# Feature attention and a maxout network on one core: unit 0's k and q set up apart, maxima of q as a row from unit 2 on, and a new order table

## The chip, the cores and the metric

One core of one Trainium2 chip runs the whole kernel. Its engines are TensorE (PE in the profile, with PEld for its weight loads), VectorE (DVE), ScalarE (ACT), GpSimd (POOL) and SyncE (SP, which issues transfers). The metric is the device time of one execution in microseconds; of several runs the median is taken. The profiled execution has a time of its own, and its span, from the first to the last instruction, is a little shorter.

## What is computed

```python
def phi(x):                                   # x: 8 batches, 8 heads, 576 tokens, 64 channels
    proj = einsum('bhsd,df->bhsf', x, w_phi)  # 128 features
    proj = proj - max(abs(proj), axis=-1)
    return concatenate([exp(proj), exp(-proj)], axis=-1)
q_p, k_p = phi(q), phi(k)
kv = einsum('bhsf,bhsd->bhfd', k_p, v);  z = sum(k_p, axis=2)
num = einsum('bhsf,bhfd->bhsd', q_p, kv)
den = einsum('bhsf,bhf->bhs', q_p, z) + 1e-6
x = num / den                                 # heads side by side: 4608 tokens of 512
h = maximum(maximum(x @ w1, x @ w2), x @ w3)  # 512 to 768
out = h @ w_out                               # 768 to 512
```

Each token of q and of k is thus projected to 128 features, and the largest absolute projection of that token is taken off ahead of both exponentials. Matrix products are in bf16 with fp32 sums.

## The kernel before

**Units.** Four heads of one batch are a unit; there are 16 units, two to a batch. A unit holds 18 tiles of 128 tokens, worked in groups of four tiles and one group of two (GROUPS). attention(u) makes the steps of a unit, each with a kind that the code names:

- L: loads. Units 0 to 3 have q and k loaded by GpSimd's queue as bf16 (line 460), and later units in fp32 by SP's. Unit 0's k comes in two halves in fp32 by SP (449), and VectorE copies it to bf16 (453, kind C). v comes in fp32 by SP (471). For units 1 to 3 a gate stands ahead of v: a one-element copy on VectorE (469), without which SP's queue does not go on.
- T and Tc: tokens and channels are exchanged. In units 0 to 3 TensorE does this (491), for q and k of a tile in one step, into a PSUM bank, and a copy brings them to qkT (494): q's channels in partitions 0 to 63, k's in 64 to 127. Later units use a transposing DMA (506).
- G: the projections with w_phi, into one bank for q (psq) and one for k (psk) (533), q and k alternating; the last two tiles share one bank (528). w_phi itself is loaded twice by SP, once for each half of the partitions (407, 408), and VectorE copies it to bf16 (403, 404).
- ek and r: ScalarE takes the two exponentials of k's projections (546); VectorE takes the maxima of the absolute values (552) of k (mk) and of q (mqp).
- E, va, vd: ScalarE makes exp(-max) of k from mk (584); GpSimd scales v by it (588) to vab, one copy for each of the two exponentials, and a small copy adds the factor itself (598).
- M and eq: q's projections once more, now with features in partitions and the maximum already subtracted (bank psm), and their exponentials on ScalarE (626). The maximum is subtracted in one of two ways. By products: a first product (615), and one small product for each tile (618), whose weights are a column of maxima spread wide and whose other operand is minus the identity. By a row: TensorE turns the maxima (560, kind R), a copy (564) and a DMA (568, kind V) put them as one more row, number 64, into qkT, and one product of 65 rows with w_phi and a row of -1 does all (613). SUBT tells from which unit on the row is used. The DMA is issued by ScalarE's queue for units below V_ACT, and by SP's for the others.
- K, N, x, X: kv sums (642), their copies kv_sb (647), numerators and denominators (660), the division on VectorE (666, 667), and the turn to xT (680, 683).

The network works in chunks of 512 tokens: chunk() makes ups (713), the maximum in hT (719, 721, 723), and the output (741, 746, 754). Its weights come by GpSimd's queue (421) and are prepared in steps of their own: differences of weights (788), turned weights (800, 803), and the product of w1 and w_out (814, 818).

**What sets the order.** Every step is a Node with costs for each engine that may do it. The order is a table written out (PLAN): each word has the number of a node, a letter for the engine (T TensorE, D VectorE, A ScalarE, G GpSimd, S SyncE), the buffers that it takes, and a due time. plan() reads it and issues the nodes in the table's order, so each engine runs its steps strictly in that order; the due times do nothing on the chip, and the engines wait for each other by semaphores. fill() adds unread products: where the table leaves TensorE without a step for more than a given gap, it puts matmuls of a constant tile (idler, made at 846) into a free bank. They have no reader. WARM and SLOW tell fill() until when the smaller gap counts, and until when such products are spaced for 0.43 us each.

Of the kernel before, what the change touches and what calls it, by code (L numbers as in the profile page):

```python
# [42 lines left out]
SUBT = 4  # L43
HALVES = 1
WARM = 28.0
SLOW = 4.6
JOIN = 2
MOVE = 5
# [49 lines left out]
2D0@0.5 8S0@0.7 10S@1.3 4S@1.9 0G@0.5 6G0@1.1 7G@1.9 12S0@3.1 3D@0.8 9D@4.5 5D@5.5 11D@6.2 1G@2.8 1051G@3.2 13T1@5.9  # L98
14D0@6.7 82G1@4.0 83G@4.9 17T2@7.5 15T3@7.6 24T004500@8.0 19T67@8.4 18D@7.8 16D@8.3 22D@8.9 27D@9.5 29T12@9.1 39T3@9.3
34T64@10.3 32D@10.1 42D@10.7 37D@11.1 26A@8.6 25A@9.3 31A@9.7 21A@10.2 36A@10.9 35A@11.5 20A@12.0 33D@11.7 38D@12.3  # L100
43D@12.9 28D@13.2 23D@13.8 64T10@11.8 58T6@12.2 65A@12.5 66A@13.0 156G2@5.7 155G@6.6 1061T4@13.0 61T1@13.6 1065T0@14.1
55T5@14.7 52T7@15.2 41A@13.4 60A@13.7 48A0@14.2 62A@14.4 44A@14.9 59A@15.2 40A@15.7 53A@16.0 30A@16.5 57A@17.0
47A0@17.5 63A@17.6 56A@18.1 54A@18.6 49G@14.6 45G@15.7 1054G@16.8 1062D0@14.4 46G@17.6 51G@18.7 50G@19.0 1052G@20.1
84D1@15.6 1066D@15.7 86T4@16.4 90T6@16.9 88T3@17.1 87D1@17.2 89D@17.8 91D@18.4 92T110211@18.0 102T41@18.6 97T35@18.8
112T6@19.1 95D@18.6 96D@19.3 107T70@19.4 103A@19.1 113A@19.6 93A@20.0 108A@20.5 109A@21.1 85S@15.8 105D@19.9 110D@20.5
67T047@21.2 115D@21.1 100D@21.4 106D@22.0 94A@21.6 98A@22.1 104A@22.8 68A@23.3 128T31@22.3 1063T2@22.8 222G0@20.9
159T1@23.4 131T4@24.0 129A@23.7 116D@22.6 69D@23.0 111D@23.3 121A1@24.2 114A@24.4 123G1@24.6 124G@25.7 101D@24.0
137T7@24.6 130A@24.7 139A@25.2 117A@25.6 99A@25.8 138A@26.3 118G@26.0 119G@27.1 122G@28.2 125T0@24.8 132A@26.6
133A@27.3 120A@27.8 134T6@25.3 136A@27.9 135A@28.6 126A@29.0 127A@29.7 223G@29.3 76T30@25.8 1053G@30.2 1057G@31.0
1055G@33.1 1064D@24.6 160D2@25.7 74T2@26.1 70T5@26.5 77D0@26.3 71D1@27.0 75D0@27.6 1071T1@26.8 157D2@28.3 1072D@28.4  # L110
# [157 lines left out]
def fill(order, spare, make, ready):  # L268
# [8 lines left out]
    for n in order:  # L277
# [3 lines left out]
        while gap > (0.35 if t < WARM else 0.5) and t < n.start - 0.2:  # L281
            for i in range(len(pool.last)):
                if all(x[0] != i or x[2] < t - 0.1 or x[1] > t + 0.6 for x in spans.values()):
                    todo.append((t, make(i)))
                    spans[t] = [i, t, t + 0.5]
                    break
# [591 lines left out]
```

## Time and profile before

| | us |
|---|---|
| median of three runs | 293.51 |
| the three runs | 292.33, 293.51, 296.66 |
| profiled execution, its own time | 292.35 |
| its span | 290.6 |
| PE busy (unread products included) | 279.4 |
| ACT busy | 189.9 |
| DVE busy | 215.9 |
| POOL busy | 117.4 |

The span is the profile's zero point to its last instruction, and times of instructions are given from its start. Busy times are sums over the span. TensorE's instructions overlap, so that the time one of them takes is longer than the distance to the next; distances between starts tell what a matmul costs in a row of them. A line of the timeline has the start, the time, engine, source line, operation, what is written and read, the number of instructions merged, and in brackets the idle time ahead of it with what ended it. The profiled execution holds 23 unread products.

### The profile page before, as it was taken

The numbers are of one execution on the slowest core, as the hardware profiler recorded it, in microseconds if no ns is written. First come the engines' busy times: TensorE is split into PE (matmuls) and PEld (weight loads), VectorE is DVE, ScalarE is ACT, GpSimd is POOL, SyncE is SP. The second block draws the span as 40 slices with busy tenths as digits, with TensorE's granted clock in tenths as the row PEclk, the third lists the DMA queues.
The fourth block names the chain that finished last, engine by engine and source line by source line (L and its number), as shares of the span: only waits on it lengthen the run. The fifth ranks groups of instructions, "written<-read, shape, count | busy, mean of one in ns | idle before, by whom it ended". The sixth has DMA issues, their size and how long they took to land.

```text
span 290.6 us, 8659 instructions
## 1 busy us (share of the span) xinstructions
PE 279.4 (96%) x3602; PEld 158.7 (55%) x3641; DVE 215.9 (74%) x457; ACT 189.9 (65%) x438; POOL 117.4 (40%) x101
## 2 busy tenths in 40 slices
PE   8878999999999999999999999999999999999993
PEld 3556685646645585564466556545555564444442
DVE  2987999998876899768989959898796583242360
ACT  1599798977988899799669797566858631120101
POOL 8086886276093751552780519107064300000000
PEclk9999999999999999999999999999999999999999
DMA  7999988997967799796995779658534523500605
GB/s 191 208 201 181 218 249 271 230 335 178 356 132 258 221 189 279 165 287 130 298 182 106 173 235 206 138 126 174 102 107 95 112 21 72 126 18 2 144 18 128
DMA packets 63051, 49.87 MB, mean 172 GB/s; under 512 B 43556, under 2 KB 48036, under 8 KB 63012
## 3 DMA queue, kind: packets, MB, share of 16 engines
q1 hardware_dynamic: 58644, 44.04, 61.2%
q0 software_dynamic: 4288, 5.21, 11.0%
q8 instruction: 28, 0.46, 0.6%
q14 instruction: 11, 0.09, 0.1%
q10 hardware_dynamic: 80, 0.07, 0.1%
HBM read 34.67 MB, written 9.44 MB: 152 GB/s over the span
## 4 chain that ended last, share of the span: by engine, by line
PE 86%; DVE 6%; ACT 4%; DMA 2%; issue 1%; SPq 0%; ACTq 0%
PE ups L713 30%; PE ops L746 16%; PE ops L741 11%; PE kvps L642 7%; PE psn L660 6%; PE psq L533 5%; PE psm L613 4%; DVE mqp L552 2%; DMA wphi_f<-in_w_phi_dram 2%; DVE mk L552 2%; ACT Ek L546 2%; PE tps L491 1%; PE pxT L680 1%; PE psm L618 1%; PE psq L528 1%
## 5 line engine op out<-in xcount | busy, mean ns | idle before, releaser
L588 POOL TENSOR_TENSOR vab<-v_raw,em 128x1152 bf16<-128x1152 f32 (+1 forms) x36 | 68.2, 1907 | 88.7 <-ACT em L584 67.7
L713 PE MATMUL ups<-xT,w_bf 128*128 128x512 bf16 x411 | 100.7, 379 | 1.1
L546 ACT ACTIVATE Ek<-psk 128x512 bf16<-128x512 f32 x128 | 70.5, 607 | 23.7 <-PE psk L533 17.0
L626 ACT ACTIVATE Eq<-psm 128x512 bf16<-128x512 f32 (+1 forms) x160 | 79.2, 586 | 7.9 <-PE psm L613 6.2
L713 PEld LDWEIGHTS <-w_bf 128*128 128x128 bf16 x432 | 40.3, 98 | 44.1 <-DVE x_sb L667 0.2
L746 PE MATMUL ops<-wout_bf,hT 128*128 128x512 bf16 (+1 forms) x219 | 50.7, 373 | 0.3
L552 DVE TENSOR_REDUCE mqp<-psq 128x4 bf16<-128x512 f32 (+1 forms) x80 | 47.7, 631 | 2.0 <-PE psk L533 1.0
L719 DVE TENSOR_TENSOR hT<-hT,ups 128x512 bf16<-128x512 bf16 x54 | 35.9, 683 | 14.2 <-ACT hT L721 6.8
L552 DVE TENSOR_REDUCE mk<-psk 128x4 f32<-128x512 f32 x64 | 42.5, 681 | 1.7 <-ACT Ek L546 1.2
L746 PEld LDWEIGHTS <-hT 128*128 128x128 bf16 x222 | 21.3, 98 | 22.8 <-DVE hT L719 0.2
L721 ACT ACTIVATE hT<-ups 128x512 bf16<-128x512 f32 x28 | 16.4, 613 | 26.2 <-PE ups L713 26.1
L667 DVE TENSOR_TENSOR x_sb<-psn,rden 128x320 bf16<-128x320 f32 x64 | 31.5, 492 | 2.2
L660 PEld LDWEIGHTS <-Eq 128*128 128x128 bf16 x640 | 24.5, 97 | 6.5 <-issue 0.3
L754 DVE COPY osb<-ops 128x512 f32<-128x512 f32 (+1 forms) x19 | 12.6, 674 | 18.9 <-PE ops L746 18.9
L660 PE MATMUL psn<-kv_sb,Eq 128*128 128x65 bf16 x640 | 26.3, 193 | 0.1
L723 DVE TENSOR_SCALAR hT<-ups 128x512 bf16<-128x512 f32 x26 | 17.5, 686 | 11.4 <-PE ups L713 11.1
L754 ACT COPY osb<-ops 128x512 f32<-128x512 f32 (+1 forms) x18 | 10.3, 575 | 23.7 <-DMA out_dram<-osb 9.6
L741 PE MATMUL ops<-xT 128*128 128x512 bf16 x86 | 24.1, 380 | 0.5
L642 PEld LDWEIGHTS <-Ek 64*128 64x128 bf16 x1152 | 18.4, 94 | 5.7 <-issue 2.8
L642 PE MATMUL kvps<-vab,Ek 64*128 64x65 bf16 x1152 | 20.5, 190 | 0.9 <-POOL vab L588 0.5
L533 PE MATMUL psq<-w,qkT 64*128 64x128 bf16 x256 | 20.4, 217 | 0.4 <-DVE qkT L494 0.4
L533 PEld LDWEIGHTS <-qkT 64*128 64x128 bf16 x512 | 14.5, 94 | 10.7 <-issue 7.7
(72 smaller groups left out, 277.8 us busy)
## 6 DMA issues: line engine op xcount, KB each, us to landing
v_raw<-in_v_dram SPq DMA_DIRECT2D x16, 576.0 KB, 4.6
out_dram<-osb SPq DMA_DIRECT2D x70, 128.0 KB, 2.4
k_raw<-in_k_dram SPq DMA_DIRECT2D x12, 576.0 KB, 4.9
q_raw<-in_q_dram SPq DMA_DIRECT2D x12, 576.0 KB, 6.1
w_bf<-in_moe_w_dram POOLq DMA_DIRECT2D x3, 768.0 KB, 10.0
qk_bf<-in_q_dram POOLq DMA_DIRECT2D x3, 288.0 KB, 10.6
qk_bf<-in_k_dram POOLq DMA_DIRECT2D x3, 288.0 KB, 11.1
wout_bf<-in_moe_w_out_dram POOLq DMA_DIRECT2D x1, 768.0 KB, 9.5
```

Source lines behind the costliest of these rows:

```text
L533: nc.tensor.matmul(ps()[:, i, :], lhsT=cols[r, :], rhs=w2[r, c, :], start=True, stop=True)
L546: nc.scalar.activation(Ek[s]()[:, tiles_of(t0, n), :], of(1), EXP, scale=1.0 - 2.0 * s)
L552: nc.vector.tensor_reduce((mq, mk)[c]()[:, tiles_of(t0, n)], of(c), AXX, ALU.max, apply_absolute_value=True)
L588: (nc.vector if n_.eng == "DVE" else nc.gpsimd).tensor_tensor(vab()[:, g, t0:t1, 0:D], vb()[:, t0:t1, :], em()[:, g, t0:t1].unsqueeze(2).t ...
L626: nc.scalar.activation(Eqb()[s][:, cols], psm()[:, 0:w], EXP, scale=1.0 - 2.0 * s)
L642: nc.tensor.matmul(kvps[ab]()[:, t // NT, g, :], lhsT=Ek[g]()[r, t, :], rhs=vab()[r, g, t, :], start=(t + g == 0), stop=(t == UT - 1 and g ...
L660: nc.tensor.matmul(psn()[:, c, :], lhsT=Eqb()[g][:, t0:t0 + P], rhs=kv()[:, pr, ab, g, :], start=(g == 0), stop=(g == 1))
L667: nc.vector.tensor_tensor(x_sb()[:, pr, :, ab, :], psn()[:, :, 0:D], rden().to_broadcast([P, 5, D]), ALU.mult)
L713: nc.tensor.matmul(ups(), lhsT=w_bf[i + 1][:, ct, j * P:(j + 1) * P], rhs=tokens_of(ct), start=(ct == 0), stop=(ct == CT - 1))
L719: nc.vector.tensor_tensor(hT()[:, j, :], hT()[:, j, :], ups(), ALU.max)
L741: nc.tensor.matmul(ops_()[:, 0:width], lhsT=tile_of(ct, tt), rhs=line_w[c_i > MOVE][:, ct, cols], start=(ct == 0), stop=False)
L746: nc.tensor.matmul(ops_()[:, 0:width], lhsT=hT()[:, j, tt * P:(tt + 1) * P], rhs=wout_bf[:, j, cols], start=False, stop=(j == JT - 1))
```

## The change

- In unit 0, k's turn (T), its copy (Tc) and its projections (G) are steps of their own, apart from q's, in banks of their own; the copies may go to ScalarE, and the table has k's three copies there and q's three on VectorE. One of the two copies of k to bf16 goes to ScalarE as well. The last two tiles of q and k still share one projection step (G). Units 1 to 15 keep q and k together.
- w_phi is loaded by ScalarE's queue, the half that k's partitions use first, behind the load of the activation table. In VectorE's order its copies to bf16 come ahead of the cast of k's second half; before they came between the two casts.
- SUBT is 2 and not 4: units 2 and 3 subtract q's maxima by the row, with the DMA on ScalarE's queue.
- fill() counts smaller gaps (0.25 and not 0.35, until 34.0 and not 28.0), spaces its products by 0.22 and not 0.26 after SLOW, puts up to two more close ahead of a step that ends a gap of over 0.6, and lets one bank serve more of them. There are 38 unread products in the program and not 23; 16 stand ahead of the first transposes and not 13.
- The table is new throughout. In its first part, SP's queue has, after the two halves of unit 0's k, unit 1's v with its gate and then unit 0's v; before, unit 0's v came right behind w_phi. GpSimd's queue has q and k of unit 1 ahead of the first network weight (before, the weight was first), and q and k of unit 2 behind GpSimd's small copy of unit 0's first factors (before, ahead of it). ScalarE's first kv copies go to VectorE.

Of the diff, the table is cut to its first lines on both sides; the changed functions are whole.

```diff
--- before.py
+++ after.py
@@ -40,11 +40,12 @@
 XW = SM + P
 BY_PE = 4
 X_PE = 6
-SUBT = 4
+SUBT=2
 HALVES = 1
-WARM = 28.0
+WARM = 34.0
 SLOW = 4.6
 JOIN = 2
+TWO_BANKS = 99
 MOVE = 5
 VA_DVE = 1
 QK = 3
@@ -95,152 +96,153 @@
 PLAN = """
-2D0@0.5 8S0@0.7 10S@1.3 4S@1.9 0G@0.5 6G0@1.1 7G@1.9 12S0@3.1 3D@0.8 9D@4.5 5D@5.5 11D@6.2 1G@2.8 1051G@3.2 13T1@5.9
-14D0@6.7 82G1@4.0 83G@4.9 17T2@7.5 15T3@7.6 24T004500@8.0 19T67@8.4 18D@7.8 16D@8.3 22D@8.9 27D@9.5 29T12@9.1 39T3@9.3
...
+8S0@0.7 10S@1.3 2D0@0.5 4A@0.7 3D@0.8 0G@0.5 6G0@1.1 7G@1.9 92G1@2.8 5D@4.6 11D@6.1 1G@3.6 9A@4.5 19T1@5.9 13T2@6.2
+17T3@6.7 21T4@6.8 15T5@7.0 23T6@7.3 14A0@6.7 20D@6.5 16A@7.6 18A@8.6 22D@7.3 24D@7.9 32T07@7.3 31T0100@7.8 26T2@8.0
+38T4@8.2 44T6@8.4 36D@8.2 35D@8.8 41D@9.5 47D@10.1 43T5@8.7 37T3@9.1 49T7@9.6 25T4@10.2 46A@9.2 33A@9.7 51A@10.2
...
@@ -278,13 +280,16 @@
         if n.eng != "PE":
             continue
         gap, t = n.start - free, max(free + 0.1, ready)
-        while gap > (0.35 if t < WARM else 0.5) and t < n.start - 0.2:
+
+        late = 2 if gap > 0.6 and t < WARM else 0
+        while gap > (0.25 if t < WARM else 0.5) and (t < n.start - 0.1 or late):
+            if t >= n.start - 0.1:
+                t, late = n.start - 0.02 * late, late - 1
             for i in range(len(pool.last)):
-                if all(x[0] != i or x[2] < t - 0.1 or x[1] > t + 0.6 for x in spans.values()):
+                if all(x[0] != i or x[2] < t - 0.1 or x[1] >= n.start for x in spans.values()):
                     todo.append((t, make(i)))
-                    spans[t] = [i, t, t + 0.5]
                     break
-            t += 0.26 if t > SLOW else 0.43
+            t += 0.22 if t > SLOW else 0.43
         free = n.start + n.costs["PE"]
     return [fn for _, fn in sorted(todo, key=lambda x: x[0])]
 
@@ -404,8 +409,8 @@
         nc.vector.tensor_copy(wphi_m[0:D, :], wphi_f[0:D, :])
 
     def phi_load():
-        nc.sync.dma_start(wphi_f[0:D, :], w_phi)
-        nc.sync.dma_start(wphi_f[D:2 * D, :], w_phi)
+        nc.scalar.dma_start(wphi_f[D:2 * D, :], w_phi)
+        nc.scalar.dma_start(wphi_f[0:D, :], w_phi)
 
     n_ident = node("const", 0, {"POOL": 0.55}, lambda: make_identity(nc, ident), [], [])
     n_minus = node("const", 0, {"POOL": 0.5}, lambda: nc.gpsimd.tensor_scalar_mul(minus, ident, -1.0), [n_ident], [])
@@ -413,8 +418,9 @@
     spare = bank("spare", [P, SM])
     n_idle = node("const", 0, {"DVE": 0.2}, lambda: nc.vector.memset(idle, 1.0), [], [spare])
     n_const = node("const", 0, {"DVE": 2.2}, zeros, [n_idle], [])
-    n_phi = node("phi", 0, {"SP": 1.2}, phi_load, [], [], pipe=0.05, lat=2.0, dmas=2)
+    n_phi = node("phi", 0, {"ACT": 1.2}, phi_load, [], [])
     n_phi = node("phi", 0, {"DVE": 0.7}, phi_weights, [n_phi, n_const], [])
+    n_phi.after = 4.6
 
     def w_load(i):
         dst = (w_bf + [wout_bf])[i]
@@ -477,27 +483,37 @@
             cast[c, 0] = nd("C", {"POOL": 0.13 + 0.055 * UT}, lambda c=c: nc.gpsimd.tensor_copy(
                 qk()[:, :, c * D:(c + 1) * D], raw_bufs(u)[c]()), [mains[c]], [(qb, kb)[c], qk])
 
-        tr = {}
+        tr, tr_of = {}, {}
 
         def tiled(t):
             return t.rearrange("p (t c) -> p t c", c=P)
         if by_pe:
-            for i, (t0, nb) in enumerate(BATCHES):
-                tps = bank("tps", [P, 8, P], BF16)
-
-                def tp(t0=t0, nb=nb, tps=tps):
-                    for n, t in enumerate(range(UT)[tiles_of(t0, nb)]):
-                        for c in range(2):
-                            nc.tensor.transpose(tps()[c * D:(c + 1) * D, n, :], qk()[:, c, t, :], ident)
-
-                def tc_(n_, t0=t0, nb=nb, tps=tps):
-                    copy_on[n_.eng](tiled(qkT())[:, tiles_of(t0, nb), :], tps()[:, 0:nb, :])
-                need = [0, 1] if nb == 2 else [i]
-                a = nd("T", {"PE": 0.056 * nb}, tp, [cast[c, j] for c in range(2) for j in need if (c, j) in cast] + [n_ident],
-                       [qk, tps], mode=2)
-                c_ = nd("Tc", {"DVE": 0.62 if nb == 8 else 0.22}, None, [a], [tps, qkT], locks=[tps])
-                c_.fn = lambda n_=c_, f=tc_: f(n_)
-                tr[i] = c_
+
+            for cs in ((1,), (0,)) if u == 0 else ((0, 1),):
+                part = {}
+                for i, (t0, nb) in enumerate(BATCHES):
+                    tps = bank("tps", [P, 8, P], BF16)
+                    rows = slice(cs[0] * D, (cs[-1] + 1) * D)
+
+                    def tp(t0=t0, nb=nb, tps=tps, cs=cs):
+                        for n, t in enumerate(range(UT)[tiles_of(t0, nb)]):
+                            for c in cs:
+                                nc.tensor.transpose(tps()[c * D:(c + 1) * D, n, :], qk()[:, c, t, :], ident)
+
+                    def tc_(n_, t0=t0, nb=nb, tps=tps, rows=rows):
+                        copy_on[n_.eng](tiled(qkT())[rows, tiles_of(t0, nb), :], tps()[rows, 0:nb, :])
+                    need = [0, 1] if nb == 2 else [i]
+                    a = nd("T", {"PE": (0.028 if u == 0 else 0.056) * nb}, tp,
+                           [cast[c, j] for c in cs for j in need if (c, j) in cast] + [n_ident], [qk, tps], mode=2)
+                    costs = {"DVE": 0.62 if nb == 8 else 0.22}
+                    if u == 0:
+                        costs["ACT"] = 0.95 if nb == 8 else 0.35
+                    c_ = nd("Tc", costs, None, [a], [tps, qkT], locks=[tps])
+                    c_.fn = lambda n_=c_, f=tc_: f(n_)
+                    part[i] = c_
+                for c in cs:
+                    tr_of[c] = part
+            tr = tr_of[0]
             un["Tc"] = tr
             for g in gates:
                 g.deps.append(units[GATES[u][0]]["Tc"][GATES[u][1]])
@@ -518,41 +534,48 @@
         for part in joined:
             given, mms = [], []
             for t0, n in part:
-                psq, psk = bank("psq", [P, 4, DF]), bank("psk", [P, 4, DF]) if n == 4 else None
+                psq, psk = bank("psq", [P, 4, DF]), bank("psk", [P, 4, DF]) if n == 4 or u >= TWO_BANKS else None
                 given.append((t0, n, psq, psk))
 
-                def proj(t0=t0, n=n, psq=psq, psk=psk):
+                def proj(cs=(0, 1), t0=t0, n=n, psq=psq, psk=psk):
                     for i, t in enumerate(range(UT)[tiles_of(t0, n)]):
                         cols = qkT()[:, t * P:(t + 1) * P]
-                        if n == 2:
+                        if psk is None:
                             nc.tensor.matmul(psq()[:, 2 * i:2 * i + 2, :].rearrange("p a f -> p (a f)"), lhsT=cols,
                                              rhs=w2.rearrange("p a f -> p (a f)"), start=True, stop=True)
                             continue
-                        for c, ps in enumerate((psq, psk)):
+                        for c in cs:
+                            ps = (psq, psk)[c]
                             r = slice(c * D, (c + 1) * D)
                             nc.tensor.matmul(ps()[:, i, :], lhsT=cols[r, :], rhs=w2[r, c, :], start=True, stop=True)
                 mms.append(proj)
             tiles = [ps for x in given for ps in x[2:] if ps]
             ti = 2 if n == 2 else t0 // NT
-            a = nd("G", {"PE": 0.22 if n == 2 else 0.236 * len(part)}, lambda mms=mms: [f() for f in mms], [tr[ti], n_phi],
-                   [qkT, mk, mq] + tiles + Ek, mode=int(n == 4))
-            projs.append(a)
-            un.setdefault("G", []).append(a)
+            if u == 0 and psk:
+                from_k = nd("G", {"PE": 0.22}, lambda f=proj: f((1,)), [tr_of[1][ti], n_phi], [qkT, mk, psk] + Ek, mode=1)
+                a = nd("G", {"PE": 0.22}, lambda f=proj: f((0,)), [tr_of[0][ti], n_phi], [qkT, mq, psq], mode=1)
+                projs += [from_k, a]
+            else:
+                need = [tr_of[c][ti] for c in range(2)] if u == 0 else [tr[ti]]
+                from_k = a = nd("G", {"PE": 0.22 if psk is None else 0.13 if n == 2 else 0.236 * len(part)},
+                                lambda mms=mms: [f() for f in mms], need + [n_phi], [qkT, mk, mq] + tiles + Ek,
+                                mode=int(psk is not None))
+                projs.append(a)
             for t0, n, psq, psk in given:
                 def of(c, n=n, psq=psq, psk=psk):
-                    return (psq, psk)[c]() if n == 4 else psq().rearrange("p (t c) f -> p t c f", c=2)[:, :, c, :]
+                    return (psq, psk)[c]()[:, 0:n, :] if psk else psq().rearrange("p (t c) f -> p t c f", c=2)[:, :, c, :]
 
                 def ex(s, t0=t0, n=n, of=of):
                     nc.scalar.activation(Ek[s]()[:, tiles_of(t0, n), :], of(1), EXP, scale=1.0 - 2.0 * s)
                 for s in range(2):
-                    exps.append(nd("ek", {"ACT": 0.49 if n == 4 else 0.34}, lambda s=s, ex=ex: ex(s), [a],
+                    exps.append(nd("ek", {"ACT": 0.49 if n == 4 else 0.34}, lambda s=s, ex=ex: ex(s), [from_k],
                                    [psk or psq, Ek[s]], locks=[psk or psq]))
                 for c in range(2):
                     def red(c=c, t0=t0, n=n, of=of):
                         nc.vector.tensor_reduce((mq, mk)[c]()[:, tiles_of(t0, n)], of(c), AXX, ALU.max,
                                                 apply_absolute_value=True)
                     ps = psk if c and psk else psq
-                    reds.append(nd("r", {"DVE": 0.607 if n == 4 else 0.34}, red, [a, n_const], [ps, (mq, mk)[c]], locks=[ps]))
+                    reds.append(nd("r", {"DVE": 0.607 if n == 4 else 0.34}, red, [(a, from_k)[c], n_const], [ps, (mq, mk)[c]], locks=[ps]))
 
         n_v, by_product = None, u < SUBT
         if not by_product:
```

## The prediction

> **What bounds the kernel now.** I read the page first: busy shares, the forty slices, then the chain that ended last. TensorE is busy for 96% of the span and 86% of the chain lies on it; the slices show where the other 4% are.
>
> ```profile
> PE 279.4 (96%) x3602; PEld 158.7 (55%) x3641; DVE 215.9 (74%) x457; ACT 189.9 (65%) x438; POOL 117.4 (40%) x101
> ...
> PE   8878999999999999999999999999999999999993
> ```
>
> The reader is to see that only the first slices (about 7.3 us each) are below 9. Busy counts unread products too (tile idler), so the first 28 us are emptier than they look. Next I asked for busy time by stretch.
>
> ```profile
> 10.00:12.00 2.00, 1.93 (x23) 0.88 (x22) 2.00 (x5) 2.00 (x5) 0.00 (x0) 1.00 1.14 203
> ...
> 16.00:20.00 4.00, 3.33 (x75) 2.20 (x72) 3.13 (x8) 4.00 (x13) 3.98 (x6) 1.00 1.05 231
> 20.00:24.00 4.00, 3.13 (x105) 2.37 (x105) 4.00 (x9) 4.00 (x11) 2.53 (x4) 1.00 1.02 144
> 24.00:28.00 4.00, 3.09 (x76) 2.51 (x72) 2.56 (x6) 4.00 (x15) 3.16 (x4) 1.00 1.14 187
> 28.00:32.00 4.00, 3.95 (x54) 2.06 (x51) 3.93 (x11) 2.86 (x6) 3.88 (x5) 1.00 1.00 193
> ...
> 100.00:140.00 40.00, 39.68 (x605) 23.70 (x610) 33.96 (x78) 35.35 (x82) 15.93 (x12) 1.00 0.91 214
> ```
>
> The columns are stretch, length, then busy time of PE, PEld, DVE, ACT, POOL. From 16 to 28 us ScalarE is busy all the time (12.00 of 12.00) and TensorE 9.55 of 12: the start is bound by ScalarE, with VectorE next. From 28 us TensorE has no hole left: 39.68 of 40 later. So two rules of pricing follow. Work taken off TensorE after 28 us is worth its full length; before 28 us, what counts is when ScalarE's and VectorE's chains begin. Those I read in the timeline of the first 16 us.
>
> ```profile
> 5.28 0.15 PEld L846 LDWEIGHTS <-idle 128*128 128x128 bf16 x1 [0.28 <-issue]
> 5.71 0.15 PEld L846 LDWEIGHTS <-idle 128*128 128x128 bf16 x1 [0.28 <-issue]
> 5.84 0.41 DVE L403 CAST w<-wphi_f 64x128 bf16<-64x128 f32 x1 [1.49 <-DMA wphi_f<-in_w_phi_dram]
> ...
> 6.70 0.80 PE L491 MATMUL tps<-ident,qk_bf 128*64 128x128 bf16 x16
> ...
> 7.43 1.04 PE L846 MATMUL idler<-idle 128*128 128x512 bf16 x4
> 7.88 0.23 DVE L403 CAST w<-wphi_f 64x128 bf16<-64x128 f32 x1 [1.64 <-DMA wphi_f<-in_w_phi_dram]
> ...
> 8.27 0.45 DVE L453 CAST qk_bf<-k_raw 128x576 bf16<-128x576 f32 x1
> ...
> 9.83 3.60 ACT L546 ACTIVATE Ek<-psk 128x512 bf16<-128x512 f32 x7 [7.82 <-PE psk L533]
> ```
>
> Unread products follow each other at 0.43 us up to 5.71 and at (1.04 - 0.39) / 3 = 0.22 us from 7.43: TensorE runs at half pace first and turns fast near 7 us, although the clock column says 1.00. VectorE waited for w_phi until 7.88, and k's second cast stood behind that, to 8.27. ScalarE's first exponential came at 9.83.
>
> **The change, part by part.**
>
> **1. The row form in units 2 and 3** (SUBT 4 to 2). It removes 2 x 34 small products (L618). What a group of four tiles costs in both forms:
>
> ```profile
> 38.59 0.38 PE L615 MATMUL psm<-qkT,w 128*128 128x512 bf16 x1
> 38.80 0.40 PE L618 MATMUL psm<-minus,mqp 128*128 128x64 bf16 x8
> 39.03 0.38 PE L615 MATMUL psm<-qkT,w 128*128 128x512 bf16 x1
> ...
> 221.83 0.97 PE psm L613 x5
> ```
>
> The first three lines are TensorE's timeline, the last is of the chain in order of time. From 38.59 to 39.03 is 0.44 us for a group with products (start to start). The row form does a whole unit, five groups, in 0.97: 4 x 0.216 + 0.11. A unit saves 4 x (0.44 - 0.216) + (0.22 - 0.11), the group of two tiles by its starts at 24.89 and 25.11, so about 1.0; two units 2.0. Added is one transpose a unit (L560); transposes at L680 go at 0.84 / 15 = 0.056 us, so 0.1 in all. Both units' products lie between 38 and 58 us, where TensorE is full: **-1.9 us**. It counts only if the new wait is covered: maxima, transpose, a copy on ScalarE (0.24, L564), a DMA on ScalarE's queue, then the products. By the table's due times the products stand 4.7 (unit 2) and 3.8 us (unit 3) behind that DMA, with other units' products and the weights' in between. Small stores land in 2.0 to 2.4 us by the page; w_phi took 5.59 (2.27 to its use at 7.88). Stall 0 at the one end, 0.9 + 1.8 = 2.7 at the other. I take 0, nearer to the stores: at 4.5 KB it is the smallest of these transfers. The issue itself stops ScalarE's queue for 0.6 (SP's issues of w_phi are 0.58 long) twice; at 36 and 51 us ScalarE bounds nothing.
>
> **2. The first transposes.** In the instruction order 16 unread products stand ahead of them, not 13. At 0.43 from 1.04 the last ends at 7.9; with the fast pace from 7.1, as here, at 7.5; if it came at 4.6, at 6.3. Before, the transposes began at 6.70. I take 7.5, by this execution's own pace.
>
> In a sentence apart: the Trainium skill, TensorE: Matmul & The Clock Gate, Part 1, lets the clock double after a window of some 3.4 us of activity that runs free of the kernel's start, so that the moment varies; the trace agrees with a late one (6 us after the first product), and no second run here shows another.
>
> **3. k apart from q.** Interleaved, q and k use two halves of the array at once: eight pairs of L533 start within 9.39 to 9.79. Apart, 32 products of 0.055 take 1.76 for 0.9, and 36 transposes (starts 0.055 apart, in pairs) 2.0 for 1.0. From 7.5: 2.0 plus one unread product of 0.22, so the first projection is at 9.7; before 9.39. Three copies of 64 rows go to ScalarE, 0.9 each for 1024 columns (512 take 0.49 between starts in L546, so 0.43 more) and about 0.35 for the short one: k's first transposes end at 8.4, the copies at 9.5, 10.7 and 11.1, and the first exponential, whose products stand behind 16 of q, starts near 11.4. **ScalarE's chain begins 1.6 us later than at 9.83.** Against this, VectorE no longer copies k, and ScalarE hands VectorE and GpSimd three copies of kv (0.38 each, L647). Bounds for the start: if the clock turns at 4.6 everything moves 1.2 earlier and the copies handed over give 1.1, so -0.7; whole lateness, +1.6. I take **+1.4**, near the upper end, since ScalarE's 12.00 of 12.00 shows no slack and part 5 comes to much the same.
>
> **4. w_phi on ScalarE's queue, first on VectorE.** The table load there ends at 2.00, so issues at 0.7 to 2.0 and 1.3 to 2.6 against 1.65 and 2.27. No longer behind k in SP's queue and no longer beside w1 and v, it should land well before 7.5, when the transposes need k's second cast. I cost it at 0; its cover is part 2, and it is lost if w_phi lands after 7.
>
> In sentences apart: the Trainium skill, Trainium Kernel Development and Optimization, Key Constraints, says that queues of several engines share the same 16 DMA engines and that a second one saves only issue time. The row has no test of that; it is rival C.
>
> **5. Loads.** Unit 0's v leaves SP at 2.90 before; now it stands behind unit 1's v, which waits for a one-element copy on VectorE (the gate), after seven of VectorE's reductions. My clock for that: projections from 9.7, first reduction 10.4, five at 0.6 and two at 0.35 make 14.1, gate, issues at 14.3 and 14.9. v lands 4.6 us after issue by the page's median, so near 19.5 to 20; four scaled copies (1.16 each, L588) and a weight issue (0.83) later unit 0's kv products can start: 25.4, not 21.1. On TensorE, some 2.0 us of work (three and a half groups of unit 1, 1.5, and eight weight transposes, 0.45) now stand ahead of them, and before they waited to 21.68: late by 25.4 - 21.7 - 2.0 = 1.7. That is the same stretch as part 3's lateness, reached by another way, and not in addition. On GpSimd q and k of unit 1 pass w1; those of unit 2 fall behind a copy that waits for ScalarE, to about 16, and need 5 to 10 us; they are due at 25.
>
> **6. More unread products**, 38 for 23, 12 more after the first transposes: 0 where TensorE waits anyway, 12 x 0.22 = 2.6 if none does. Nearly all stand before 28 us; I take **+0.2**, one product that comes at the wrong moment.
>
> **Sum**, against the profiled execution's own 292.35 us (span 290.6): -1.9 + 1.4 + 0.2 = -0.3, so 292.05. The three runs have 292.33, 293.51 and 296.66, the profiled one at their lower end; I add 0.35 for that, a third of the way to the median: **292.4**.
>
> **Rivals.** A, the start costs nothing: clock early, ScalarE relieved by the copies handed over; -1.9 - 0.7 + 0.2 = -2.4, 290.3. For it: VectorE's 3.1 us of waits for w_phi go. Against it: 16 products at 0.43.
>
> B, slower: unit 0's v. If it lands as late as the slowest v of the timeline (issue 29.66, landed 7.6 later) at 22.5, kv starts at 28.0, late by 28.0 - 21.7 - 2.0 = 4.3. Sum -1.9 + 4.3 + 0.2 = +2.6: 295.3 with the same 0.35. It decides from a landing of about 20, where the start's loss passes the 1.7 that is left of the gain. For it: DMA engines at 1.0 to 1.2 of their time in these stretches. Against it: w1 should have landed by 15.
>
> C, w_phi lands as long after issue as before (4.2 and 5.6): 6.2 and 8.2; k's second cast ends at 9.3, the remaining transposes and copies move back by 1.0: 293.4. This is where the skill's rule leads; against it stands that w1 and v are no longer in flight.
>
> **How the numbers follow.** Forecast 0.5, A 0.15, B 0.17, C 0.13, other 0.05. The forecast's own range is 291.4 to 293.4. For 8 in 10 I take 290.2 to 295.3: A inside, and B up to its price. A measurement of this kernel tells about 2% (5.9 us) from no change; only a stall of both row waits on top of B would pass it: slower 0.03; faster 0.01, since even A gives 0.8%; within 0.96.
>
> **What would show it.** Right: the first transposes near 7.5, the first exponential near 11.4, kv products of unit 0 near 25, row-form groups at 0.22 in units 2 and 3 with no idle TensorE before them, and no holes after 30 us. Wrong: first exponential before 10 (A), v landing past 20 (B), VectorE waiting for w_phi past 7 (C), or TensorE idle before the row's products around 41 and 55 us.

## The result: 303.75 us, and the profile after

| | before | after |
|---|---|---|
| median, us | 293.53 | 303.75 (302.71 to 304.89, 4 runs) |
| ratio to before, 95% | | 1.0341 [1.0257, 1.0424] |
| profiled execution, its own time | 292.35 | 302.71 |
| its span | 290.6 | 300.9 |

The changed kernel is 3.4% slower, 10.2 us by the medians. The forecast was 292.4 with a range of 290.2 to 295.3. All four runs lie above the range, and the case given 0.03 came true.

The page of the kernel after, first its busy times and slices, then the chain that ended last and the group of the unread products:

```profile
PE 287.4 (96%) x3549; PEld 159.6 (53%) x3590; DVE 209.5 (70%) x447; ACT 197.0 (65%) x450; POOL 117.5 (39%) x104
...
PE   7997999999999999999999999899999999999993
...
PEclk9999799999999999999999999999999999999999
...
PE ups L736 31%; PE ops L769 15%; PE ops L764 10%; PE psn L683 7%; PE kvps L665 6%; PE idler L869 6%; PE psq L550 5%; PE psm L636 5%; PE tps L501 2%; PE pm L837 2%; PE psq L544 1%; PE pxT L703 1%; PE psm L638 1%; PE psm L641 1%; PE psk L550
...
L869 PE MATMUL idler<-idle 128*128 128x512 bf16 x38 | 18.6, 489 | 3.8 <-DVE mqp L575 1.1
```

TensorE is as busy as before by its share (96%), and 8.0 us busier by its sum. The unread products alone are 6% of the chain: they now stand on the path that sets the end. And the clock row, all 9 before, has a 7 in the fifth slice. Where that falls, and how little real work TensorE does at that time, the busy time by stretch shows (columns as in the prediction):

```profile
28.00:32.00 4.00, 2.65 (x10) 0.60 (x6) 4.00 (x9) 3.27 (x9) 2.51 (x3) 0.77 1.18 184
32.00:36.00 4.00, 3.94 (x111) 3.14 (x109) 0.69 (x2) 1.95 (x7) 4.00 (x6) 0.80 1.17 209
36.00:40.00 4.00, 3.89 (x88) 2.57 (x79) 3.40 (x9) 3.21 (x10) 4.00 (x4) 1.00 0.84 128
40.00:100.00 60.00, 59.37 (x933) 36.09 (x944) 56.12 (x118) 50.44 (x118) 34.23 (x25) 1.00 0.90 248
```

From 28 to 32 us TensorE finishes 10 matmuls (54 before) at a granted clock of 0.77. From 36 us on it is full, 59.37 of 60 later. Nearly all of the loss is thus made before 36 us. TensorE's timeline of that time:

```profile
1.04 10.21 PE L869 MATMUL idler<-idle 128*128 128x512 bf16 x16 [1.04 <-DVE idle L419]
...
4.91 0.11 PEld L869 LDWEIGHTS <-idle 128*128 128x128 bf16 x1 [0.53 <-issue]
...
11.18 1.50 PE L501 MATMUL tps<-ident,qk_bf 128*64 128x128 bf16 x16
...
12.61 0.61 PE L869 MATMUL idler<-idle 128*128 128x512 bf16 x1
...
13.14 0.90 PE L501 MATMUL tps<-ident,qk_bf 128*64 128x128 bf16 x20
...
15.57 1.09 ACT L569 ACTIVATE Ek<-psk 128x512 bf16<-128x512 f32 x2 [0.21 <-PE psk L550]
...
29.29 2.73 PE L869 MATMUL idler<-idle 128*128 128x512 bf16 x5 [1.13 <-DVE mqp L575]
...
34.89 1.27 PE L665 MATMUL kvps<-vab,Ek 64*128 64x65 bf16 x72
```

The reader is to see the first line: 16 unread products take 10.21 us, 0.64 each, where 13 took 5.73 before. The weight load between two of them stands idle for 0.53 (0.28 before). The first transposes therefore come at 11.18 and not at 6.70, ScalarE's first exponential at 15.57 and not at 9.83, and unit 0's kv products at 34.89 and not at 21.1. At 29.29 five more unread products begin, after a wait of 1.13 us for VectorE's reader of a bank, and the next real product comes only behind them, at 32.07. The fast pace comes late too: the single product at 12.61 still lasts 0.61 us, and only the transposes from 13.14 are fast. Before, the pace turned near 7.1.

**The cause, as read from the code.** The diff removes one line of fill(), `spans[t] = [i, t, t + 0.5]`. It was the note that bank i is taken by an unread product until t + 0.5. Without it each product finds the first free bank free again, so all of a row of them get the same one, and each then waits until the one ahead has ended. That wait is read from the code and from the distances; the profile puts the idle time down to "issue" and names no releaser. With banks in turn, products overlap: 0.43 from start to start, though one of them lasts 0.63 (the longest of before's). In one bank the distance is the whole duration, 0.60, and 0.04 more.

### The profile page after: what moved, and what is told of

The parts are those of the page before. It is cut to its first block, busy times and chain, and to the rows that moved or that the text cites. A ratio compares the mean times of both kernels' runs of the same rounds, so it can differ in the third digit from the quotient of the medians.

```text
span 300.9 us, 8576 instructions
## 1 busy us (share of the span) xinstructions
PE 287.4 (96%) x3549; PEld 159.6 (53%) x3590; DVE 209.5 (70%) x447; ACT 197.0 (65%) x450; POOL 117.5 (39%) x104
## 4 chain that ended last, share of the span: by engine, by line
PE 94%; issue 2%; DVE 1%; ACT 1%; ACTq 0%
PE ups L736 31%; PE ops L769 15%; PE ops L764 10%; PE psn L683 7%; PE kvps L665 6%; PE idler L869 6%; PE psq L550 5%; PE psm L636 5%; PE tps L501 2%; PE pm L837 2%; PE psq L544 1%; PE pxT L703 1%; PE psm L638 1%; PE psm L641 1%; PE psk L550 1%
## 5 line engine op out<-in xcount | busy, mean ns | idle before, releaser
L736 PE MATMUL ups<-xT,w_bf 128*128 128x512 bf16 x411 | 99.7, 379 | 1.2
L649 ACT ACTIVATE Eq<-psm 128x512 bf16<-128x512 f32 (+1 forms) x160 | 78.4, 588 | 10.5 <-PE psm L636 7.1
L569 ACT ACTIVATE Ek<-psk 128x512 bf16<-128x512 f32 x128 | 71.7, 616 | 12.8 <-PE psk L550 7.2
L777 ACT COPY osb<-ops 128x512 f32<-128x512 f32 (+1 forms) x24 | 13.9, 586 | 34.5 <-PE ops L769 23.3
L744 ACT ACTIVATE hT<-ups 128x512 bf16<-128x512 f32 x32 | 18.9, 615 | 20.2 <-PE ups L736 20.0
L746 DVE TENSOR_SCALAR hT<-ups 128x512 bf16<-128x512 f32 x22 | 14.7, 685 | 14.2 <-PE ups L736 14.2
L869 PE MATMUL idler<-idle 128*128 128x512 bf16 x38 | 18.6, 489 | 3.8 <-DVE mqp L575 1.1
L550 PEld LDWEIGHTS <-qkT 64*128 64x128 bf16 x512 | 15.3, 94 | 12.9 <-issue 9.8
L550 PE MATMUL psk<-w,qkT 64*128 64x128 bf16 x256 | 20.2, 217 | 1.4 <-ACT kv_sb L670 1.1
L636 PE MATMUL psm<-qkT,wphi_m 128*128 128x512 bf16 (+1 forms) x70 | 20.4, 358 | 0.0
```

What stands on the lines that cost most here:

```text
L550: nc.tensor.matmul(ps()[:, i, :], lhsT=cols[r, :], rhs=w2[r, c, :], start=True, stop=True)
L569: nc.scalar.activation(Ek[s]()[:, tiles_of(t0, n), :], of(1), EXP, scale=1.0 - 2.0 * s)
L636: nc.tensor.matmul(psm()[:, 0:w], lhsT=wphi_m, rhs=rhs, start=True, stop=True)
L649: nc.scalar.activation(Eqb()[s][:, cols], psm()[:, 0:w], EXP, scale=1.0 - 2.0 * s)
L736: nc.tensor.matmul(ups(), lhsT=w_bf[i + 1][:, ct, j * P:(j + 1) * P], rhs=tokens_of(ct), start=(ct == 0), stop=(ct == CT - 1))
L869: nc.tensor.matmul(idler, lhsT=idle, rhs=idle.unsqueeze(1).to_broadcast([P, 4, P]), start=True, stop=True)
```

## The experiments

Theory: the time went into unread products, first by the shared bank (0.64 and not 0.43 us each), then by their number. Rivals: the new order (k apart, v late, w_phi on another queue), and the row form's waits. Unread products have no reader, so a kernel without them leaves nothing of the output out.

| run | edit | median, us | ratio to before, 95% |
|---|---|---|---|
| after | | 303.75 | 1.0341 [1.0257, 1.0424] |
| a_rot | after, banks in turn | 298.22 | 1.0147 [1.0092, 1.0202] |
| a_rot13 | a_rot, 13 first products | 297.24 | 1.0139 [1.0086, 1.0191] |
| a_rot_nolate | a_rot without the two extra ones | 293.79 | 1.0011 [0.9980, 1.0041] |
| a_none | after, no unread products | 293.13 | 0.9993 [0.9962, 1.0025] |
| a_oldfill | after with before's fill() | 292.13 | 0.9953 [0.9925, 0.9982] |
| a_oldfill_onebank | a_oldfill without the removed line | 294.97 | 1.0052 [1.0024, 1.0079] |
| a_oldfill_subt4 | a_oldfill, SUBT 4 | 293.41 | 1.0004 [0.9967, 1.0041] |
| a_oldfill_phisp | a_oldfill, w_phi by SP | 292.45 | 0.9985 [0.9960, 1.0010] |
| a_oldfill_v0first | a_oldfill, order unchanged | 291.94 | 0.9947 [0.9919, 0.9975] |
| a_oldfill_v0at2 | a_oldfill, v of unit 0 early | 294.93 | 1.0059 [1.0026, 1.0092] |
| b_onebank | before without the removed line | 300.26 | 1.0193 [1.0122, 1.0264] |
| b_newfill | before with after's fill() | 305.94 | 1.0404 [1.0343, 1.0465] |

Before itself took 292.81 to 293.80 in these comparisons. Differences between runs of different chips are taken from the ratios, times 293.5. By the two intervals such a difference is uncertain by some 1 to 3 us.

**1. Is it the unread products or the order?** a_oldfill gives the changed kernel the fill() of before and WARM 28 (16 products in all, 13 first); a_none leaves them all out; b_newfill does the reverse and gives the kernel before the new fill() and WARM 34 (49 products, 16 first). The first and the last are the change's own diff of fill(), one way or the other; a_none's is:

```diff
-        while gap > (0.25 if t < WARM else 0.5) and (t < n.start - 0.1 or late):
+        while False and gap > (0.25 if t < WARM else 0.5) and (t < n.start - 0.1 or late):
```

> The changed kernel with the filling rule of before (16 unread products, 13 ahead of the first transposes, banks taken in turn) and its limit of 28.0. Theory 1: first transposes near 6.7, time 292 to 295, a little under the version with 38 in turn, as fewer products stand in the way. Theory 2: 300 or above.

> The changed kernel without any unread product. Theory 1: first transposes when q has landed, near 6, and no waits behind products, but TensorE stays at half pace longer, as nothing keeps it busy; 292 to 298. Theory 2: 300 or above, as the order is the same.

> The kernel before, its own order and row setting, with the changed kernel's filling rule (49 unread products, 16 ahead of the first transposes, always the first free bank). Theory 1 (the filling rule is what costs, and it costs in any order): 303 to 307, as in the changed kernel. Theory 2 (the rule hurts only in the new order, whose gaps it fits badly): under 298.

Measured: 292.13, 293.13 and 305.94. The whole loss goes with fill(): the new table with the old fill() is 0.5% under before, and the old table with the new fill() is 4.0% over it. The rivals of the new order fall as causes of the loss. TensorE's and ScalarE's timeline of a_oldfill, for comparison with after's:

```profile
1.04 4.39 PE L866 MATMUL idler<-idle 128*128 128x512 bf16 x13 [1.04 <-DVE idle L416]
...
6.58 1.59 PE L498 MATMUL tps<-ident,qk_bf 128*64 128x128 bf16 x36 [1.15 <-DMA qk_bf<-in_q_dram]
...
7.50 2.19 ACT L501 COPY qkT<-tps 64x1024 bf16<-64x1024 bf16 x3 [3.00 <-PE tps L498]
...
9.90 1.09 ACT L566 ACTIVATE Ek<-psk 128x512 bf16<-128x512 f32 x2 [0.21 <-PE psk L547]
...
20.21 3.38 POOL L608 TENSOR_TENSOR vab<-v_raw,em 128x576 bf16<-128x576 f32 x3 [2.75 <-DMA v_raw<-in_v_dram]
...
25.58 0.69 PE L662 MATMUL kvps<-vab,Ek 64*128 64x65 bf16 x34 [0.90 <-POOL vab L608]
```

Here TensorE is ready for the transposes at 5.4 and waits 1.15 for q's transfer. All 36 transposes take 1.59, and the first exponential comes at 9.90.

**2. How much is the shared bank?** a_rot keeps the new fill() and its 38 products, and only chooses the banks in turn. b_onebank and a_oldfill_onebank take the line out of kernels that had it (25 and 19 products come out then, for 23 and 16).

```diff
-            for i in range(len(pool.last)):
+            for i in [(len(todo) + j) % len(pool.last) for j in range(len(pool.last))]:
```

```diff
                     todo.append((t, make(i)))
-                    spans[t] = [i, t, t + 0.5]
                     break
```

> The changed kernel with one edit: its 38 unread products take the free banks in turn, not always the first free one. Theory 1 (each product waits for the one before it, as both write one bank): 0.43 us between starts at half pace, not 0.64, so the 16 ahead of the first transposes end by 7.9 and not at 11.2; the later groups of 3 to 5 shrink by half too; time 294 to 297. Theory 2 (the new order starts late by itself, through ScalarE's chain and unit 0's v): the time stays at 300 or above, with kv products of unit 0 past 30 us as in the changed kernel (34.9).

> The kernel before with one line taken out, so that unread products all go to the first free bank as in the changed kernel. Theory 1: the 13 ahead of the first transposes take 0.64 each, 2.8 us more, and the first transposes start near 9.4 and not 6.7; 1 to 3 us of it reach the end: 294.5 to 296.5. Theory 2: no change, 293.5, since only the order costs.

> The changed kernel with the filling rule of before but for the one line that moves products on from bank to bank (19 products, 13 first). Theory 1: 13 x 0.21 = 2.8 us later at the first transposes (9.3 against 6.6) and some of the clock's full pace lost; 295 to 299. If the wait on one bank were covered, 292.

Measured: a_rot 298.22, b_onebank 300.26, a_oldfill_onebank 294.97. From the ratios, the shared bank costs 5.7 us in after (1.0341 less 1.0147), 5.7 in before (1.0193), and 2.9 in a_oldfill (1.0052 less 0.9953). The line alone thus makes before slower by 1.9% [1.2%, 2.6%]. Both a_rot and b_onebank came out slower than expected: b_onebank's 294.5 to 296.5 counted only the 13 first products at 0.21 us each. First a_rot's timeline, then that of a_oldfill_onebank:

```profile
1.04 6.54 PE L869 MATMUL idler<-idle 128*128 128x512 bf16 x16 [1.04 <-DVE idle L419]
...
7.73 0.86 PE L501 MATMUL tps<-ident,qk_bf 128*64 128x128 bf16 x16
...
11.40 1.09 ACT L569 ACTIVATE Ek<-psk 128x512 bf16<-128x512 f32 x2 [0.22 <-PE psk L550]
```

```profile
1.04 8.29 PE L865 MATMUL idler<-idle 128*128 128x512 bf16 x13 [1.04 <-DVE idle L415]
...
9.26 1.97 PE L497 MATMUL tps<-ident,qk_bf 128*64 128x128 bf16 x36
...
13.08 1.08 ACT L565 ACTIVATE Ek<-psk 128x512 bf16<-128x512 f32 x2 [0.21 <-PE psk L546]
```

With banks in turn the 16 first products take 6.54, and with one bank 13 of them take 8.29, 0.64 each again. The pace also turns later with one bank, by the times of single products and transposes: near 10.2 in a_oldfill_onebank and 13 in after, against 4.0 to 7.1 in the kernels with banks in turn. The profiled executions of b_onebank and b_newfill (302.93 and 309.84 us, above their medians) have it near 16 and 18. So the shared bank costs more than the longer row of first products; how much of the 5.7 us is due to the late pace was not measured apart.

**3. How much is the number of products?** a_rot_nolate takes the up to two extra products ahead of a step out of a_rot (30 products, 14 first). a_rot13 has only the first products cut to 13 (35 in all).

```diff
-        late = 2 if gap > 0.6 and t < WARM else 0
+        late = 0
```

```diff
-        late = 2 if gap > 0.6 and t < WARM else 0
-        while gap > (0.25 if t < WARM else 0.5) and (t < n.start - 0.1 or late):
+        late = 2 if gap > 0.6 and t < WARM and free else 0
+        while gap > (0.25 if t < WARM else 0.5) and (t < n.start - (0.1 if free else 0.4) or late):
```

> The changed kernel with banks in turn, but without the up to two extra products close ahead of a step (30 products, 14 of them first). If those extra ones are what delays: 294 or less. If the plain filling of smaller gaps does it: 296 or more.

> The changed kernel with banks in turn, and 13 unread products ahead of the first transposes, not 16; the other 22 stay (35 in all). Theory 1a (what is left of the loss, 298.2 against 292.1 with the old filling rule, is the three more at half pace): 293 or less. Theory 1b (it is the 22 later ones, which stand in gaps of the start's order and make TensorE late, or wait for a reader of their bank): 296 or more.

Measured: 293.79 and 297.24. The extra products cost 4.0 us (1.0147 less 1.0011). The three more at the start cost only 0.2 by the ratios, 1.0 by the medians, which the intervals do not tell from nothing, although ScalarE's first exponential is 1.85 us later with them (11.40 against 9.55). Their two profiled executions are no clean pair: in a_rot13's the granted clock falls to 0.69 and 0.89 between 24 and 32 us, and unit 0's kv products come at 29.17, later than a_rot's 28.52. From a_rot13 to a_oldfill, both with 13 first products, 22 later ones become 3 and 5.5 us go: 0.29 us for each of the 19 (0.2 to 0.4 by the intervals, where one costs 0.22 in a row). So a product in a gap is not free here.

How such a product costs time shows where TensorE waits for VectorE's maxima. First a_none, then a_rot at the same place of the order:

```profile
22.24 0.58 PE L638 MATMUL psm<-qkT,w 128*128 128x512 bf16 x1 [0.88 <-DVE mqp L575]
```

```profile
24.68 1.89 PE L869 MATMUL idler<-idle 128*128 128x512 bf16 x5 [1.13 <-DVE mqp L575]
26.41 0.38 PE L638 MATMUL psm<-qkT,w 128*128 128x512 bf16 x1
```

Without unread products the real product itself waits 0.88 us. With them the wait is still there, and the row runs behind it and not in it: 1.73 us to the next real product for five in a_rot, 1.07 for three in a_rot_nolate (22.09 to 23.16), 0.43 for one in a_oldfill (20.86 to 21.29). The kv products of unit 0 follow: 28.52 in a_rot, 26.7 in a_rot_nolate, 23.93 and (second half, after a wait for GpSimd) 25.58 in a_oldfill. How all of the 4.0 us of the extra ones arises is not settled. The two kernels' profiled executions (296.67 and 295.35) lie closer together than their medians, and a_rot_nolate's has a stretch at a lower clock that a_rot's lacks (0.84 and 0.73 in 20 to 28 us, some 1.7 us of lost clock).

**4. What is the row form worth?** a_oldfill_subt4 sets SUBT back to 4, and the six steps of the row in units 2 and 3 leave the table.

```diff
-SUBT=2
+SUBT=4
```

> The changed kernel with the old filling rule and the row form undone in units 2 and 3 (SUBT 4 again, same order but for the six steps that fall away). The prediction's part 1: 1.9 us of TensorE come back, so 294.0 against 292.1. Rival: the row's waits had eaten the gain, or the products are hidden: 292.1 again.

Measured: 293.41 against 292.13; by the ratios the row form is worth 1.5 us, give or take 1.4. Unit 2 in TensorE's timeline, first of a_oldfill, then of a_oldfill_subt4 (of this one the first group and the last):

```profile
42.12 1.14 PE L633 MATMUL psm<-qkT,wphi_m 128*128 128x512 bf16 x5
```

```profile
41.50 0.38 PE L633 MATMUL psm<-qkT,w 128*128 128x512 bf16 x1
41.72 0.40 PE L636 MATMUL psm<-minus,mqp 128*128 128x64 bf16 x8
...
43.07 0.38 PE L633 MATMUL psm<-qkT,w 128*128 128x512 bf16 x1
43.29 0.40 PE L636 MATMUL psm<-minus,mqp 128*128 128x64 bf16 x8
```

Five groups in 1.14 us against 2.19 (41.50 to 43.69), and no idle time stands ahead of the row's products.

**5. w_phi's queue.** a_oldfill_phisp has SP issue w_phi's two loads again; they fall between k's halves there.

```diff
-        nc.scalar.dma_start(wphi_f[D:2 * D, :], w_phi)
-        nc.scalar.dma_start(wphi_f[0:D, :], w_phi)
+        nc.sync.dma_start(wphi_f[0:D, :], w_phi)
+        nc.sync.dma_start(wphi_f[D:2 * D, :], w_phi)
```

> The changed kernel with the old filling rule and w_phi's two loads issued by SP behind k's halves, as before. The prediction's part 4 (cover until 7): w_phi lands near 5 to 6 since v and w1 are no longer in flight, and the time stays at 292.1. Rival C: it lands as long after issue as before, VectorE's cast of k moves past 8, 293 or more.

Measured: 292.45 against 292.13; by the ratios 0.9 us, with intervals that overlap. The first exponential moves from 9.90 to 10.86, since the transposes now wait 0.80 us for k's second cast: the load of k's second half leaves only at 2.45, behind w_phi's two issues of 0.58 us each. The Trainium skill, Trainium Kernel Development and Optimization, Key Constraints, says that a further queue saves only issue time, the DMA engines being shared; 0.9 us, or 0.3 by the medians, is no more than those two issues and agrees with that.

**6. Unit 0's v early.** a_oldfill_v0first moved v's word to the head of the table and left its due time; a_oldfill_v0at2 changed the due time.

```diff
-138T2@22.9 147T4@23.4 1079T0@23.6 1082D@23.0 12S2@12.8 140A@23.9
+138T2@22.9 147T4@23.4 1079T0@23.6 1082D@23.0 12S2@1.9 140A@23.9
```

> The changed kernel with the old filling rule and unit 0's v issued by SP right behind k, as before, and not behind unit 1's gated v. The prediction's part 5 and rival B: v lands by 10, the scaled copies no longer wait for it, unit 0's kv products start 1 to 2 us earlier, 291 against 292.1. If that lateness is covered by the order (other work stands ahead of them), or the early transfer delays q instead: 292 to 293.

> This is the changed kernel with the unread products of before, and with unit 0's v issued on SP's queue right behind k (its due time 1.9 in place of 12.8), so that unit 1's v and its gate come after it; this time the order itself is changed. Theory (part 5: v lands late, the scaled copies wait for it 2.75 us and TensorE's kv products of unit 0 wait for the copies): the scaled copies start without a wait for v, unit 0's kv products come 1 to 3 us earlier, and the time is 290.0 to 291.5, against 292.1 with v late. Rival 1, the stretch is held by ScalarE, which is busy 11.97 of 12 us from 16 to 28: the kv products come earlier but the time stays at 291.8 to 292.5. Rival 2, v takes transfer time from q, w_phi or w1 in the first 10 us: first exponential later than 9.90, time 292.5 to 293.5.

The first edit changed nothing: fill() returns all steps sorted by due time, so on every engine the order stayed as it was. The description of the kernel above is wrong in saying that the due times do nothing on the chip: they set the order. That run is a repeat of a_oldfill, and gives 291.94 for 292.13.

The second edit did move v, and cost 3 us: 294.93, by the ratios 3.1 more than a_oldfill. Rival 2 holds, with more than its price. Its timeline, and its stretch from 8 to 12 us:

```profile
7.13 0.46 DVE L405 CAST w<-wphi_f 64x128 bf16<-64x128 f32 x2 [5.15 <-DMA wphi_f<-in_w_phi_dram]
...
7.78 3.05 PE L498 MATMUL tps<-ident,qk_bf 128*64 128x128 bf16 x36 [2.11 <-DMA qk_bf<-in_q_dram]
...
12.36 1.08 ACT L566 ACTIVATE Ek<-psk 128x512 bf16<-128x512 f32 x2 [0.21 <-PE psk L547]
...
19.92 3.38 POOL L608 TENSOR_TENSOR vab<-v_raw,em 128x576 bf16<-128x576 f32 x3
```

```profile
8.00:12.00 4.00, 4.00 (x58) 3.67 (x57) 2.30 (x5) 2.14 (x3) 0.00 (x0) 0.60 1.19 214
```

v no longer keeps GpSimd waiting, but q lands 1.2 us later (the transposes start at 7.78 for 6.58), and after a wait of 2.11 us for it TensorE runs the transposes at a granted clock of 0.60: 3.05 us for 36 against 1.59. Unit 0's kv products start at 26.4, not earlier. So v late was the better place. Most of the loss goes with the clock: averaged over their executions the granted clock is 0.9885 here and 0.9968 in a_oldfill, and 0.0083 of 291 us is 2.4 us of the 3.1, an estimate that takes all lost clock as lost time. The profiled execution, at 0.993, is only 0.4 us slower than a_oldfill's.

**The sum of the parts**, by ratios: one bank 5.7, the later products 5.5, three more first products 0.2, and the rest of the change (a_oldfill) -1.4: together 10.0 us of 293.5. The runs form a chain from after to before, so these parts must add up, and the sum is no test of them. Of the rest, the row form, w_phi's queue and v's place were undone one by one; k apart and the new order of GpSimd's queue were not.

## Why the prediction was wrong, point by point

**What bounds the kernel.** That TensorE is full from 28 us, and that work taken off there counts in full, fits: the row form gave 1.5 of the 1.9. That before 28 us only the start of ScalarE's and VectorE's chains counts was wrong for TensorE's products there; for the chains the runs do not agree (part 3).

**Part 2, the first transposes: the step that failed.** "At 0.43 from 1.04 the last ends at 7.9; with the fast pace from 7.1, as here, at 7.5." The instruction order gave the right number, 16; the spacing was taken from before, where the products had banks in turn. In one bank it is 0.64, the fast pace taken at 7.1 came near 13, and the transposes came at 11.18. With banks in turn, in a_rot, they came at 7.73. What the diff removed was printed, and its effect on the banks was not worked out. The price was in the trace of before: one product lasted up to 0.63 us there while the next began after 0.43, so a wait for its end adds 0.2. The Trainium skill, TensorE: Matmul & The Clock Gate, Single matmul latency, gives (219 + N) / 1.2 ns at half rate and (398 + N) / 2.4 at full, an estimate of 609 and 379 ns for 512 columns; the traces agree with 600 to 607 and 380 to 390 ns for one product in a shared bank, and set 30 to 50 ns on top for the wait.

**Part 6, more unread products: the other step that failed.** "+0.2, one product that comes at the wrong moment", with a bound of 12 x 0.22 = 2.6. The later products cost 5.5 with banks in turn, for 19 of them; 12 would cost 3.5 in proportion. The small term assumed that nearly all of them fall into time in which TensorE waits anyway. They stand in such gaps of the table, but on the chip they ran behind the wait, as 24.68 in a_rot shows. The count also took before's ten later products as free; no run takes those out.

**Part 3, k apart.** The mechanism was right, and the time nearly: the first exponential was to come 3.9 us after the first transposes, and came 3.7 after them in a_rot and 3.3 in a_oldfill. That a_rot has 11.40 for 11.4 is luck in part, as its transposes were 0.2 late. The price is less sure: "+1.4, near the upper end, since ScalarE's 12.00 of 12.00 shows no slack". Between a_rot and a_rot13 the first exponential differs by 1.85 us and the time by 0.2 to 1.0; a_none, with its first exponential at 10.98, has 293.13. In a_oldfill, ScalarE's chain begins at 9.90, and what the row form leaves of its -1.4 is about 0 for this term; no run undoes the split of k by itself. Lateness beyond that does show: 0.96 us in a_oldfill_phisp goes with 0.9 us of time, within its error, and 3.18 in a_oldfill_onebank (13.08) with 2.9, beside three more products.

**Part 1, the row form.** Predicted -1.9 with no stall; measured -1.5, or -1.3 by the medians. From start to start unit 2's products took 0.97 us (42.12 to 43.09) for 2.02, so 1.05 less, as the sum had it. The row's DMA leaves at 37.36 and its products start at 42.12: the cover was there.

**Part 4 and rival C, w_phi.** Costed at 0; 0.9 by the ratios in a_oldfill_phisp, 0.3 by the medians, and not clear of 0. VectorE's first cast of w_phi came at 5.37 in a_oldfill and at 6.13 in after, before the 7 that rival C needs; in a_rot it came at 7.62, with k's second cast at 8.23 and the first exponential still at 11.40.

**Part 5 and rival B, unit 0's v.** "25.4, not 21.1" was the start. In a_oldfill 38 of the 72 kv products started at 23.93 and the other 34 at 25.58; GpSimd's copies waited 2.75 for v, to 20.21, as the working had it (19.5 to 20). That it costs little beside the rest held: a_oldfill is 0.5% faster than before in spite of it, and v moved ahead costs 3.1. In after v was not what kv waited for: GpSimd waited 0.17 for it, at 24.38.

**Rival A** (the start costs nothing, 290.3) is nearest to what the change without its fill() does: 292.13, -1.4 and not -2.4.

**The chances.** All cases were built on the order of the steps, and none on fill(); 0.05 was left for "other". A rival that ends slower should have asked what a changed line in the filler does to every product that it makes.

## What to carry to other kernels

Price a row of matmuls by what each waits for: with a bank of its own it costs the distance between starts, in a shared bank where it waits for the one ahead its whole duration, here (128x512) half as much again at half pace and double at full pace. Products that only keep TensorE busy are work like any other once the order is fixed: no such products at all (293.13) was 3.5% better than 38 in one bank, and 16 by the old rule (292.13) only 0.3% better than none, 0.4% by the ratios, with intervals that overlap. When a planner's bookkeeping changes, look at which buffer and which wait each instruction gets, not only at their number and order; the version to keep here is the change with the old fill().

## What the runs showed of the hardware that was not expected

- Products into one bank, each waiting for the one ahead: 0.64 us from start to start at half pace and 0.43 at full pace. In turn: 0.43 and 0.22. A row of them in one bank also kept the half pace longer (10.2 and 13 us for 4.0 to 7.1).
- The pace fell back to half in the middle of the start. In after, the chain of waits in order of time shows products at the two paces within one row:

```profile
29.29 0.39 PE idler L869
29.72 0.39 PE idler L869
30.15 0.60 PE idler L869
30.79 0.60 PE idler L869
31.43 0.60 PE idler L869
32.07 0.58 PE psm L638
```

  It had been fast since about 13, and no wait that is listed for TensorE before it is longer than 1.13 us. The Trainium skill, TensorE: Matmul & The Clock Gate, HAM oscillation, speaks of idle gaps above some 3.4 us; here it happened with much shorter gaps, TensorE being busy for 3.22 of 4 us from 24 to 28 and 2.65 from 28 to 32. It happened too at 20 to 28 us in a_rot_nolate (0.84 and 0.73) and a_none (0.78 and 0.79), and at 24 to 32 in a_rot13. What brings it about is open: a_rot kept the full clock behind the same wait of 1.13 us, and a_oldfill with TensorE busy for only 2.91, 2.71 and 2.65 of 4 us from 16 to 28.
- The mean granted clock of an execution goes with its time. Of the 87 executions of the kernel before in these comparisons, the 24 with 0.998 or more have a median of 292.5 us, the 23 below 0.992 one of 295.7. Before a difference of 1 or 2 us is put down to a change, the clocks of its executions are to be compared.
- The moment of the fast pace varies between kernels whose first products take banks in turn: near 4.0 in a_oldfill, 5.1 in a_rot13, 7.1 in a_rot and before. It varies within one order too: a_oldfill_v0first, in a_oldfill's order, turned near 5.3. Without any unread products, in a_none, it came near 15.5, and that kernel is still only 1.0 us slower than a_oldfill.
- A load issued earlier can cost more than a load issued late: with v at 1.65 us on SP's queue q landed at 7.78, for 6.58 and 6.50 in a_oldfill and a_none. w_phi's cast came at 7.13 for 5.37, but it came at 7.62 in a_rot without an early v, so that part is not shown.
